# Another order of early loads, visits and blocks in a retention and squared-ReLU feed-forward kernel

## The chip, the cores and the metric

The kernel runs on one core of one Trainium2 chip. The metric is the device time of one execution in microseconds (us). The kernel before took 210.53 us, the median of 8 runs (209.96 to 211.82).

## What is computed

Eight heads of a linear recurrence with decay, then a feed-forward network on the result:

```python
gamma = 1.0 - 2.0 ** (-5.0 - np.arange(H))
for t in range(S):
    state = gamma[None, :, None, None] * state + np.einsum('bhd,bhe->bhde', k[:, :, t], v[:, :, t])
    y[:, :, t] = scale * np.einsum('bhd,bhde->bhe', q[:, :, t], state)
x = y.transpose(0, 2, 1, 3).reshape(B * S, H * D)
h = np.maximum(x @ w_in, 0.0)
out = h * h @ w_out
```

with B = 4, H = 8, S = 768, D = 64; w_in is 512 x 2048 and w_out 2048 x 512. All inputs and the output are float32; the kernel multiplies in bfloat16.

## The kernel before

**Work and its names.** The 3072 tokens are 24 chunks of 128, numbered 0 to 23, six for each batch entry. The recurrence is done by chunks, in halves of 64 tokens. What a chunk m needs is loaded by three DMAs (`ldk`, `ldq`, `ldv`, lines 436 and 616), cast to bfloat16 on whatever engine the plan gives (`ck`, `cq`), and v is scaled on VectorE (`cv`, line 627). q and k must also be transposed. Chunks 0 to 3 go in pairs (`together`, `pair_visits`, 512 KB a load, steps T, E, A, B, C); chunks 4 and 5 by TensorE with a copy out of PSUM (`Tk`, `Tq`, `Ek`, `Eq`); chunks from NPE = 6 to below NTD by `flips` inside a visit (32 transposes of 64 x 64 into the upper half of the tile `yy`, line 642, and one ScalarE copy `E`, line 648); all later ones by a DMA transpose `X` that SyncE issues (line 660).

**Visits.** A visit `Vm.n` on TensorE finishes chunk m (`values`, `apply`: tile `yy`) and begins chunk n (`scores`, `sums`: tile `sc`); `V.5` only begins, `V4.` only finishes. After it VectorE masks the scores (`Pn`, line 766), adds up the states (`Sn.0`, `Sn.1`, lines 777 and 779) and scales the result into the network's input (`Ym`, line 788, which reads `yy`). The next visit needs P and S of its m, and the transposed q and k of its n.

**The network.** `BLOCKS` groups the chunks: FFN1 of a block (`F1.b.f`, line 835) runs 64 matmuls, each 128 columns wide per chunk of the block, in groups of one PSUM bank of 512; ScalarE applies the ReLU (`R`, line 840), VectorE squares (`Q`, line 845). FFN2 of a chunk (`F2.m.0` to `.3`, line 880) runs 16 matmuls of 512 columns in four pieces; ScalarE copies the result out (`Om`, line 888) and SyncE stores it (`stm`, line 893). w_in comes in four half-blocks and two whole ones (`ldwin0` to `5`), w_out in four (`ldwout0` to `3`), each cast to bfloat16 in parts (`cw`).

**Who sets the order.** [...]each engine runs its list from first to last. The list is made while the kernel is built, by `Plan.schedule`: it places, one by one, the operation that could start earliest by its own estimates, and among equals the one of lower priority number. `ORDER` gives the loads' priorities, `HOME` fixes an operation's engine, `RANK` its priority; `LEAD` and `PACE` set how far ahead of FFN1 the visits stand, `F2LAG` how far FFN2 stands behind; `AHEAD` is how many chunks ahead a chunk's preparation is written into the plan, `PRE` a number of tiny matmuls at the start, and fillers (line 936) are matmuls on the identity put where TensorE would be idle early on. Nearly all DMAs stand in one list on SyncE's queue: loads, transposes and stores. The order of the built instructions on each engine was compared for both kernels; places in it that the next sections name come from there.

Of the kernel before, what the change touches and what calls it, by code (L numbers as in the profile page):

```python
# [18 lines left out]
class Plan:  # L19
# [12 lines left out]
    BLOCK = 256  # L32
    AHEAD = 50
    HOP = 0.15
# [6 lines left out]
    def add(self, name, eng, dur, reads=(), writes=(), fn=None, prio=0.0, lat=0.0, bank=None, after=(), count=0):  # L41
# [17 lines left out]
        else:  # L59
            flex = True  # L60
        if name in HOME:
            eng = {HOME[name]: eng[HOME[name]]}
        prio = RANK.get(name, prio)
        self.ops.append(dict(i=i, name=name, eng=eng, flex=flex, deps=sorted(deps), fn=fn,
# [3 lines left out]
    def schedule(self, nbanks, max_open):  # L68
# [18 lines left out]
        if "PE" in eng_free:  # L87
            eng_free["PE"] = 0.06 * PRE
        bank_free = [0.0] * nbanks
# [7 lines left out]
        done = 0  # L97
        issued, edge, next_fetched, history, crossed = 2 * PRE, self.BLOCK0, 3.0, [], 0.0
        while done < n:
# [54 lines left out]
            else:  # L154
                if eng == "PE":
# [9 lines left out]
                    while issued + todo > edge:  # L165
                        step = max(0, edge - issued)
                        now = max(now + step * per, next_fetched)
                        issued, todo = max(issued, edge), todo - step
                        ahead = next((y for x, y in reversed(history) if x <= edge - self.AHEAD), 0.0)
                        ahead = max(ahead, crossed)  # L170
# [5 lines left out]
                    history.append((issued, t + dur))  # L176
                    if any(before < x <= issued for x in range(self.BLOCK0 - self.AHEAD, issued + 1, self.BLOCK)):
                        behind = [x for x in moves if x[0] > t + 0.4]
# [35 lines left out]
TURN = (0.60, 1.10, 16, 2.4)  # L214
WIDE = (0.60, 2.80, 33, 0.6)
STORE = (0.30, 0.80, 9, 0.6)
BLOCKS = [2, 2, 1, 1, 2, 2, 2, 4, 4, 4]
SPLIT = 6
AHEAD = 5
WARM = 20.0  # L220
FILL = 0.215
WARMING = 18.4
PACE = 10
LEAD = 1
NPE = 6
NTD = 8
PRE = 50
WHALF = 2
WHALFD = (0.60, 1.47, 33, 0.6)
CVT = {'DVE': 0.69, 'POOL': 1.3}  # L230
TCAST = {'DVE': 0.43, 'ACT': 0.63, 'POOL': 0.78}
TEVAC = {'ACT': 0.6, 'DVE': 0.62}
NPAIR = 2
F2LAG = 5.0
F2WAIT = 4
LAST = [256, 128, 128]
CAST = {"k": {"DVE": 0.43, "ACT": 0.63, "POOL": 0.78}, "q": {"DVE": 0.43, "ACT": 0.63, "POOL": 0.78}}
# [2 lines left out]
WPRIO = {"in": -2.0, "out": 2.0}  # L240


HOME = {'cq7': 'ACT', 'ck7': 'DVE', 'ck4': 'ACT', 'cwout0.1': 'POOL', 'cwin1.0': 'ACT', 'cq0.0': 'DVE', 'Ek2.0': 'DVE', 'cwout2.0': 'ACT', 'ck2.1': 'POOL', 'cwin5.3': 'DVE', 'ck5': 'ACT', 'cq6': 'ACT', 'Eq5': 'ACT', 'cwin3.0': 'ACT', 'ck6': 'DVE', 'cwout1.0': 'DVE', 'ck0.0': 'DVE', 'cwin4.0': 'DVE', 'cwout3.3': 'ACT', 'cwin1.2': 'DVE', 'cwin5.0': 'DVE', 'Ek0.1': 'ACT', 'cwout1.2': 'POOL', 'cwin2.0': 'ACT', 'cwout0.2': 'DVE', 'cwin4.2': 'DVE', 'cwin5.2': 'POOL'}
ROUND = []
RANK = {'P0.00': -1.1, 'Tk2.1': 21.9, 'vf20': -1.1, 'B0': 1.9, 'S1': 0.9, 'Y2.0': 5.65}
ORDER = (
    "k0 q0 v0 k2 o0 q2 o1 v2 i0 i1 o2 i2 k4 i3 i4 i5 q4 v4 k5 q5 o3 q6 k6 v5 q7 v6 v7 k7"
)


# [8 lines left out]
def kernel(  # L259
# [25 lines left out]

    blocks = BLOCKS
    assert sum(blocks) == NM
# [318 lines left out]
    def prepare(m):  # L606
        if m < 2 * NPAIR:
            if m % 2 == 0:
                together(m // 2)
            return  # L610
        b, i = where(m)
        slot = m % NLD
        for x in "kqv":
            t = ld[x][:, slot, :]
            pl.add(f"ld{x}{m}", "SP", SMALL, (), (f"ld{x}{slot}",),
                   lambda x=x, t=t: nc.sync.dma_start(
                       t.rearrange("s (h d) -> s h d", h=H),
                       src[x][b, :, i * C : (i + 1) * C, :].rearrange("h s d -> s h d")),
                   prio=dma_prio[(x, m)])
        for x in "kq":  # L620
            t, o = ld[x][:, slot, :], bf[x][m % NBF]
            pl.add(f"c{x}{m}", CAST[x], 0, (f"ld{x}{slot}",), (f"bf{x}{m % NBF}",),
                   lambda on, t=t, o=o: copy_on(on, o.rearrange("s j a d -> s a j d"),
                                                t.rearrange("s (a j d) -> s a j d", a=2, j=NJ)), prio=urgency(m))
        t, o = ld["v"][:, slot, :], bf["v"][m % NBF]
        pl.add(f"cv{m}", "DVE", 0.69, (f"ldv{slot}", "vf"), (f"bfv{m % NBF}",),
               lambda: nc.vector.tensor_tensor(  # L627
                   out=o[:], in0=t.rearrange("s (h d) -> s h d", h=H),
                   in1=vf[:, i, :, None].to_broadcast([P, H, D]), op=ALU.mult),
               prio=urgency(m))  # L630
# [21 lines left out]
    def transpose(m):  # L652


        qkT, t = qkts[m % NQT], kq[m % NBF]
        if m < 2 * NPAIR or NPE <= m < NTD:
            return
        if m >= NPE:
            pl.add(f"X{m}", "SP", TURN, (f"bfk{m % NBF}", f"bfq{m % NBF}"), qkeys(m),
                   lambda: nc.sync.dma_start_transpose(out=qkT.rearrange("p x j t -> p (x j) t"),  # L660
                                                       in_=t.rearrange("s x j a d -> s (x j a d)")), prio=-0.5)
            return
        for x, name in enumerate("kq"):
            o1 = {}

            def fn(x=x, o1=o1):
                ps = fps[o1["op"]["bank_index"]].bitcast(BF16)
                for j in range(NJ):
                    nc.tensor.transpose(ps[:, j * P : j * P + P], t[:, x, j].rearrange("s a d -> s (a d)"), ident[:])  # L669
            i0 = pl.add(f"T{name}{m}", "PE", 0.26, (f"bf{name}{m % NBF}", "ident"), (f"gT{name}{m}",), fn,  # L670
                        prio=-200 + m, lat=0.2, count=4, bank=("open", ("T", m, x), False))
            o1["op"] = pl.ops[i0]
            pl.add(f"E{name}{m}", EVAC, 0, (f"gT{name}{m}",), (qkeys(m)[x],),
                   lambda on, x=x, o1=o1: copy_on(on, qkT[:, x].rearrange("p j t -> p (j t)"),
                                                  fps[o1["op"]["bank_index"]].bitcast(BF16)[:, 0:512]),
                   prio=urgency(m), lat=0.05, bank=("close", ("T", m, x)))
# [50 lines left out]
    def visit(m, n, t=None):  # L727
# [28 lines left out]
        if n is None:  # L756
            dur += 0.2
        pl.add(f"V{'' if m is None else m}.{'' if n is None else n}", "PE", dur, reads, writes, fn,
               prio=-300 + n if m is None else -300 + m if m < PACE else (m - LEAD) * 8, lat=0.25,
               count=32 * ((m is not None) + (n is not None) + (t is not None)) + 1)  # L760
# [99 lines left out]
    def ffn2(blk):  # L860
        for q4 in range(blk0[blk], blk0[blk] + blocks[blk]):
# [5 lines left out]
            for part, w in enumerate(widths):  # L867
# [5 lines left out]
                for j in range(4):  # L873
                    reads = [f"h{g % NH2}.{u}.{4 * j + c}" for c in range(4)] + [f"wout{j}.{c}.{h}" for c in range(4) for h in range(2)]

                    def mm(j=j, o1=o1, h2=h2, u=u, ns=ns, w=w):
                        ps = fps[o1["op"]["bank_index"]]
                        for c in range(4):
# [3 lines left out]
                    i0 = pl.add(f"F2.{q4}.{j}" + f"/{part}" * (parts > 1), "PE", 0.866 * w / DM, reads, (f"g{grp}",), mm,  # L882
                                prio=(q4 + F2LAG) * 8 + 2 * j + 1 + part * 9, lat=0.2,
                                bank=("open", grp, True) if j == 0 else ("use", grp), count=4)
# [18 lines left out]
    for m in range(-1, NM):  # L903
        n = m + 1
        for x in range(0 if m < 0 else m + AHEAD, min(NM, m + AHEAD + 1)):
            prepare(x)
            transpose(x)
        t = m + 2 if NPE <= m + 2 < NTD else None
        if n < 2 * NPAIR:
# [18 lines left out]
    if tc is not None:  # L928
        with tc.manual_schedule():
            one = nc.const_aps.tensor(1.0, [P, 1], BF16)  # L930
            for _ in range(PRE):
                nc.tensor.matmul(fps[NBANK - 1][0:1, 0:1], lhsT=one, rhs=one, start=True, stop=True)
# [37 lines left out]
```

## Time and profile before

| | |
|---|---|
| runs | median 210.53 us, 209.96 to 211.82, 8 runs |
| the profiled execution | 210.22 us; span of its instructions 208.4 us |
| mean granted TensorE clock | 0.992 |
| HBM read, written | 27.26 MB, 6.29 MB |
| DMA queue of the loads, stores and transposes | 80.5% of 16 engines' span |
| FFN1 matmuls (L835) | 640, of 128, 256 and 512 columns |
| FFN2 matmuls (L880) | 416 |
| transposes by DMA (L660) | 16; flips (L642): 64 matmuls |

The profile is that of one execution. Its page gives, for each engine, the busy time, then the span in 40 slices whose digits are busy tenths, then the chain of work that ended last: from the last instruction back, at each step, to what released it. PE is TensorE, PEld its weight loads, DVE VectorE, ACT ScalarE, POOL GpSimd and SP SyncE; L and a number is the line of the kernel. In a timeline a row has the start, the duration, the engine, the line, the operation, the tiles (out<-in), and in brackets how long its engine was idle before it and what ended that. When a DMA landed is seen where a waiting engine goes on with that as its releaser, and in the trace's semaphore events. Successive matmuls overlap in the profile, so a group's time is better read from its first matmul to that of the next group.

### The profile page before, as it was taken

What the parts mean: (1) busy time and instruction counts of PE and PEld (TensorE: products, weight loads), DVE (VectorE), ACT (ScalarE), POOL (GpSimd) and SP (SyncE); (2) the same over time, 40 slices, a digit from 0 to 9 for tenths busy, and PEclk for the clock granted to TensorE, in tenths of its full rate; (3) what the DMA queues carried; (4) which work ended last, traced back from release to release, by engine and by line L of the source; (5) the groups of instructions that cost most, each with busy time, mean ns of one, the idle gap of its engine ahead of it and who ended that gap; (6) DMA issues with size and microseconds to landing.
All of it is one profiled execution on the core that took longest, in us unless ns stands there. A gap on an engine that the chain in (4) does not pass through costs nothing.

```text
span 208.4 us, 6170 instructions
## 1 busy us (share of the span) xinstructions
PE 201.8 (97%) x2687; PEld 120.9 (58%) x2687; DVE 113.4 (54%) x249; ACT 91.5 (44%) x154; POOL 39.2 (19%) x67
## 2 busy tenths in 40 slices
PE   7979999999999999999999999999999999999994
PEld 5655787664484776857744444444444444444453
DVE  2597688655294684746763657935668324320000
ACT  8443777385341452533511465213653136532121
POOL 6652224310221122221302222202300000000000
PEclk9996999999999999999999999999999999999999
DMA  6999999999999999999969999889920110011212
GB/s 162 290 318 324 380 324 371 264 251 206 285 195 195 247 191 217 217 159 234 172 154 264 193 235 192 157 184 210 212 53 0 53 50 3 0 50 52 101 53 101
DMA packets 94587, 38.15 MB, mean 183 GB/s; under 512 B 79968, under 2 KB 88544, under 8 KB 94560
## 3 DMA queue, kind: packets, MB, share of 16 engines
q1 hardware_dynamic: 94416, 37.69, 80.5%
q8 instruction: 21, 0.34, 0.7%
q10 hardware_dynamic: 144, 0.07, 0.1%
q14 instruction: 6, 0.05, 0.1%
HBM read 27.26 MB, written 6.29 MB: 161 GB/s over the span
## 4 chain that ended last, share of the span: by engine, by line
PE 89%; DMA 4%; SPq 4%; ACT 1%; issue 1%; DVE 0%; POOL 0%; ACTq 0%
PE fps L835 41%; PE fps L880 40%; DMA wst<-in_moe_w_in_dram 4%; SPq L436 4%; PE yy L686 2%; PE yy L701 2%; PE sc L723 1%; PE sc L712 1%; ACT qkT L648 0%; PE fps L669 0%; PE yy L642 0%; DVE xt L788 0%; POOL w_in L421 0%; PE sc L522 0%; PE yy L522 0%
## 5 line engine op out<-in xcount | busy, mean ns | idle before, releaser
L835 PE MATMUL fps<-xt,w_in 128*128 128x256 bf16 (+2 forms) x640 | 89.0, 297 | 0.8 <-DVE xt L788 0.4
L880 PE MATMUL fps<-w_out,h 128*128 128x512 bf16 (+2 forms) x416 | 88.2, 363 | 0.0
L840 ACT ACTIVATE h<-fps 128x512 bf16<-128x512 f32 x96 | 57.3, 597 | 42.0 <-PE fps L835 41.8
L835 PEld LDWEIGHTS <-w_in 128*128 128x128 bf16 x640 | 57.3, 99 | 29.2 <-issue 0.7
L845 DVE TENSOR_TENSOR h<-h 128x512 bf16<-128x512 bf16 x96 | 42.8, 455 | 35.7 <-ACT h L840 35.5
L880 PEld LDWEIGHTS <-h 128*128 128x128 bf16 x416 | 38.0, 98 | 39.1
L888 ACT ACTIVATE osb<-fps 128x512 f32<-128x512 f32 (+2 forms) x26 | 14.7, 564 | 56.6 <-PE fps L880 56.6
L788 DVE TENSOR_TENSOR xt<-yy,yf 128x512 bf16<-128x512 f32 x20 | 13.8, 688 | 25.6 <-PE yy L701 21.8
L421 POOL CAST kqs<-kn 128x512 bf16<-128x512 f32 x16 | 10.6, 660 | 64.5 <-DMA kn<-in_k_dram 58.9
L421 POOL CAST kqs<-qn 128x512 bf16<-128x512 f32 x17 | 11.2, 660 | 22.7 <-DMA qn<-in_q_dram 20.6
L627 DVE TENSOR_TENSOR vs<-vn,vf 128x512 bf16<-128x512 f32 x20 | 13.7, 687 | 2.6 <-DMA vn<-in_v_dram 2.6
L779 DVE TENSOR_TENSOR state<-sc,state 128x256 bf16<-128x256 f32 x33 | 13.8, 419 | 0.5
L766 DVE TENSOR_TENSOR pt<-sc,cmask 128x512 bf16<-128x512 f32 x20 | 13.6, 681 | 0.3 <-PE sc L723 0.3
L701 PE MATMUL yy<-qkT,state 64*64 64x64 bf16 x296 | 9.9, 198 | 0.2
L686 PEld LDWEIGHTS <-vs 64*64 64x64 bf16 x320 | 4.2, 107 | 7.1 <-issue 7.0
L936 PE MATMUL fps<-ident 128*128 128x256 bf16 x29 | 6.8, 379 | 0.0
L686 PE MATMUL yy<-pt,vs 64*64 64x64 bf16 x320 | 6.3, 198 | 0.0
L701 PEld LDWEIGHTS <-state 64*64 64x64 bf16 x296 | 6.1, 107 | 0.4 <-PE yy L701 0.4
L723 PE MATMUL sc<-vs,kqs 64*64 64x64 bf16 x288 | 6.2, 193 | 0.0
L712 PE MATMUL sc<-qkT 64*64 64x64 bf16 x320 | 6.2, 193 | 0.0
L421 POOL CAST w_in<-wst 128x512 bf16<-128x512 f32 x6 | 4.0, 678 | 10.2 <-DMA wst<-in_moe_w_in_dram 10.2
L421 POOL CAST w_out<-wst 128x512 bf16<-128x512 f32 x6 | 4.0, 690 | 8.9 <-DMA wst<-in_moe_w_out_dram 8.9
(70 smaller groups left out, 92.3 us busy)
## 6 DMA issues: line engine op xcount, KB each, us to landing
out_dram<-osb SPq DMA_DIRECT2D x23, 256.0 KB, 2.6
kn<-in_k_dram SPq DMA_DIRECT2D x20, 256.0 KB, 4.6
qn<-in_q_dram SPq DMA_DIRECT2D x20, 256.0 KB, 4.4
vn<-in_v_dram SPq DMA_DIRECT2D x20, 256.0 KB, 4.7
wst<-in_moe_w_out_dram SPq DMA_DIRECT2D x4, 1024.0 KB, 10.3
wst<-in_moe_w_in_dram SPq DMA_DIRECT2D x4, 512.0 KB, 8.0
wst<-in_moe_w_in_dram SPq DMA_DIRECT2D x2, 1024.0 KB, 9.1
kn<-in_k_dram SPq DMA_DIRECT2D x2, 512.0 KB, 7.1
```

What stands on the lines that cost most here:

```text
L421: nc.gpsimd.tensor_copy(o, t)
L627: lambda: nc.vector.tensor_tensor(out=o[:], in0=t.rearrange("s (h d) -> s h d", h=H), in1=vf[:, i, :, None].to_broadcast([P, H, D]), op=AL ...
L686: nc.tensor.matmul(yy[L * c : L * c + L, sub, p * L : p * L + L], lhsT=vs[r, 4 * a + j, :], rhs=pt[r, a, j, :], start=(p == 0), stop=True, ...
L701: nc.tensor.matmul(yy[L * c : L * c + L, sub, p * L : p * L + L], lhsT=st[r, j, :], rhs=qkT[r, 1, j, sub * L : sub * L + L], start=False, ...
L766: lambda: nc.vector.tensor_tensor(out=pt[:], in0=sc[:, :, 0:256].rearrange("s g (p t) -> s g p t", p=NJ), in1=cmask[:, None, None, :].to_b ...
L779: f = lambda cc=cc, j1=j1, j0=j0: nc.vector.tensor_tensor(out=sts[j1][:], in0=cc, in1=sts[j0][:], op=ALU.add)
L788: lambda: nc.vector.tensor_tensor(out=xt[:, :, u * C : u * C + C].rearrange("s p (g t) -> s g p t", g=2), in0=yy[:, :, 0:256].rearrange("s ...
L835: nc.tensor.matmul(ps[:, u * n : u * n + n], lhsT=w_in_bf[j][:, cb, c * P : (c + 1) * P], rhs=xt[:, cb, cols], start=(cb == 0), stop=(cb = ...
L840: nc.scalar.activation(h2[:, f0 : f0 + per, cols], ps[:].rearrange("p (u n) -> p u n", u=per), AF.Relu)
L845: nc.vector.tensor_mul(hv, hv, hv)
L880: nc.tensor.matmul(ps[:, 0:w], lhsT=h2[:, fb, u * C : u * C + C], rhs=w_out_bf[j][:, c, ns], start=(fb == 0), stop=(fb == NFB - 1))
L888: lambda o1=o1, slot=slot, ns=ns, w=w: nc.scalar.activation(osbs[slot][:, ns], fps[o1["op"]["bank_index"]][:, 0:w], AF.Copy),
```

## The change

Only constants of the plan change. The first loads become k0 q0 v0 q2 k2 v2, then three half-blocks of w_in, then q4, w_in, k4 and so on; NTD 7 sends chunk 7 through the DMA transpose; chunks 12 to 15 become two blocks of two; the visits' lead is two chunks, a chunk is prepared four ahead, FFN2's lag is 3.5; 20 tiny matmuls at the start instead of 50; other places for casts and copies; no fixed priorities.

```diff
-BLOCKS = [2, 2, 1, 1, 2, 2, 2, 4, 4, 4]
+BLOCKS = [2, 2, 1, 1, 2, 2, 2, 2, 2, 4, 4]
 SPLIT = 6
-AHEAD = 5
+AHEAD = 4
...
-PACE = 10
-LEAD = 1
+PACE = 8
+LEAD = 2
 NPE = 6
-NTD = 8
-PRE = 50
+NTD = 7
+PRE = 20
...
-F2LAG = 5.0
+F2LAG = 3.5
...
-HOME = {'cq7': 'ACT', 'ck7': 'DVE', 'ck4': 'ACT', 'cwout0.1': 'POOL', 'cwin1.0': 'ACT', 'cq0.0': 'DVE', 'Ek2.0': 'DVE', 'cwout2.0': 'ACT', 'ck2.1': 'POOL', 'cwin5.3': 'DVE', 'ck5': 'ACT', 'cq6': 'ACT', 'Eq5': 'ACT', 'cwin3.0': 'ACT', 'ck6': 'DVE', 'cwout1.0': 'DVE', 'ck0.0': 'DVE', 'cwin4.0': 'DVE', 'cwout3.3': 'ACT', 'cwin1.2': 'DVE', 'cwin5.0': 'DVE', 'Ek0.1': 'ACT', 'cwout1.2': 'POOL', 'cwin2.0': 'ACT', 'cwout0.2': 'DVE', 'cwin4.2': 'DVE', 'cwin5.2': 'POOL'}
+HOME = {'cq7': 'DVE', 'cwin1.0': 'ACT', 'Eq0.1': 'ACT', 'cwin5.2': 'POOL', 'Ek0.0': 'ACT', 'cwin4.1': 'DVE', 'ck0.1': 'POOL', 'Eq2.0': 'DVE', 'cq0.0': 'DVE', 'cwout3.1': 'ACT', 'Eq0.0': 'ACT', 'cwout2.1': 'ACT', 'cwin4.2': 'DVE', 'cwout2.2': 'ACT', 'cq5': 'POOL', 'cwin4.0': 'DVE', 'cwout3.0': 'DVE', 'cwin0.0': 'ACT', 'cwout0.3': 'POOL', 'cwout1.0': 'DVE', 'cwout2.3': 'POOL'}
 ROUND = []
-RANK = {'P0.00': -1.1, 'Tk2.1': 21.9, 'vf20': -1.1, 'B0': 1.9, 'S1': 0.9, 'Y2.0': 5.65}
+RANK = {}
 ORDER = (
-    "k0 q0 v0 k2 o0 q2 o1 v2 i0 i1 o2 i2 k4 i3 i4 i5 q4 v4 k5 q5 o3 q6 k6 v5 q7 v6 v7 k7"
+    "k0 q0 v0 q2 k2 v2 i0 i1 i2 q4 i3 i4 k4 i5 v4 o0 q5 o1 k5 o2 o3 q6 v5 k6 v6 q7 k7 v7"
 )
```

In ORDER, i is a piece of w_in and o a piece of w_out. In the built lists SyncE's loads follow the new ORDER as written. Before, they stood as k0 q0 v0 k2 q2 v2 i0 i1 i2 k4 i3 i4 i5 q4 o0 v4 o1 o2 k5 q5 o3 q6 k6 v5 q7 v6 v7 k7, since a load whose buffer is not yet free is placed later. X7 stands on SyncE's list behind the loads of k8, q8 and v8 and the first two stores.

## The prediction

> **What bounds the kernel now.** I read the page's engine shares and its 40 slices first, then the chain of work that ended last, then the table by stage of the first 24 us, and last the timelines of VectorE and of the DMA queue around the fifth and sixth chunk. "Start to start" below means the distance between first matmuls of neighbouring pieces of work on TensorE, read from the timeline.
>
> The page, engine shares and slices (one slice is 5.2 us):
>
> ```profile
> PE 201.8 (97%) x2687; PEld 120.9 (58%) x2687; DVE 113.4 (54%) x249; ACT 91.5 (44%) x154; POOL 39.2 (19%) x67
> ...
> PEclk9996999999999999999999999999999999999999
> DMA  6999999999999999999969999889920110011212
> GB/s 162 290 318 324 380 324 371 264 251 206 285 195 195 247 191 217 217 159 234 172 154 264 193 235 192 157 184 210 212 53 0 53 50 3 0 50 52 101 53 101
> ```
>
> TensorE is full, and for the first 150 us so are the DMA engines. So two things can set the end: the sum of TensorE's work, and whatever TensorE needs that arrives late. The fourth slice has a lower clock.
>
> The chain, with the middle left out:
>
> ```profile
> 8.54 8.01 DMA wst<-in_moe_w_in_dram
> 16.60 0.62 POOL w_in L421
> 17.27 3.39 PE fps L835 x16
> ...
> 55.57 1.03 ACT qkT L648
> 56.63 0.70 DVE xt L788
> 57.37 1.95 PE fps L835 x32
> ```
>
> FFN1 cannot begin before the first half of w_in lands and is cast; from 17.27 on the chain is TensorE but for one place. At 55.57 ScalarE copies chunk 7's transposed q and k out of PSUM, and VectorE's Y5 waits for it, as the next timeline shows: 3.82 us idle. F2.4.0 starts at 55.93 and takes 0.86; F1.3.0 could follow at 56.79 and starts at 57.37: 0.58 us lost. The other lines are why Y5's engine matters: it takes its work in order, and waits for loads.
>
> ```profile
> 47.53 0.42 DVE L845 TENSOR_TENSOR h<-h 128x512 bf16<-128x512 bf16 x1
> 50.19 0.69 DVE L627 TENSOR_TENSOR vs<-vn,vf 128x512 bf16<-128x512 f32 x1 [2.25 <-DMA vn<-in_v_dram]
> 50.80 0.68 DVE L766 TENSOR_TENSOR pt<-sc,cmask 128x512 bf16<-128x512 f32 x1
> 51.40 0.41 DVE L779 TENSOR_TENSOR state<-sc,state 128x256 bf16<-128x256 f32 x1
> ...
> 56.63 0.69 DVE L788 TENSOR_TENSOR xt<-yy,yf 128x512 bf16<-128x512 f32 x1 [3.82 <-ACT qkT L648]
> ```
>
> VectorE stood until v6 landed at 50.17; P5 (L766), whose input visit V.5 had made at 48.8, came only after. V5.6 needed it at 54.12, so nobody waited.
>
> **TensorE's sum, part by part.**
> - Chunks 12 to 15 as two blocks of two instead of one of four: FFN1 turns 64 matmuls of 512 columns into 128 of 256. The chain has 52 of the first in 11.22 (216 ns each) and 72 of the second in 7.86 (109 ns): 13.81 becomes 13.98, **+0.17**. The relus and squares stay 16 of the same shape.
> - Chunk 7 by DMA: its 32 transposes leave visit V5.6, which took 0.93 start to start with them, against 0.67 for V7.8 without: **-0.26**. The ScalarE copy of 1.02 goes too, and with it Y5's wait for it: **-0.58**. What is late next there: in the built order of the changed kernel F2.3.0 and F2.3.1 (1.73) stand between V5.6 and F1.3.0, while Y5 needs about 1.1 after V5.6 and v7's scaling before it; that fits.
> - Visits moved ahead (LEAD, AHEAD, F2LAG): the same visits and groups in another order; no work.
> - 20 warm-up matmuls instead of 50, and 31 fillers instead of 29: all ahead of 17.27, hidden behind the wait for w_in. Without that cover the fillers cost 0.23 each (12 in 2.74 at the early speed); 20 now stand ahead of the first transpose, so that starts near 6.5 instead of 5.53. By FFN1 this is recovered: its gate, w_in's first half, has the same six 512 KB loads ahead of it (k2 and q2 only trade places) and lands at 16.55 again.
>
> **The first FFN1.** Before, VectorE stood from 17.02 to 18.09 for a w_in cast that was queued ahead of state S2; C2.0 ran at 20.59, after F1.0.2. In the changed order that cast is on GpSimd, S2 is done near 18.1, and C2.0 runs between F1.0.0 and F1.0.2. The stage table has the other price here:
>
> ```profile
> 16.00:18.00 2.00, 1.62 (x55) 1.33 (x54) 1.01 (x2) 0.63 (x1) 0.61 (x1) 0.88 1.12 334
> 18.00:20.00 2.00, 2.00 (x11) 1.21 (x10) 1.78 (x5) 1.23 (x2) 0.28 (x1) 0.50 1.19 289
> ```
>
> The seventh figure is the granted clock: half speed from 17.5 to 20.9, where F1.0.0 took 1.50 and F1.0.2 1.82 start to start, against 0.87 later. With it the changed order gives F1.0.0 17.3, C2.0 18.8, F1.0.2 20.1, C2.1 21.4, F1.0.4 22.1, Tq4 23.0 and F1.1.0 at 23.2, against 23.52: -0.3. [...]
>
> **The weights after that.** k4 now goes ahead of w_in's last block, q5 ahead of w_out's second, k5 ahead of its third, each a 256 KB load of about 1.05 us. By the old landings with these pieces moved: w_in's last at 29.0 instead of 27.98, cast by 30.4, read by F1.0.12 at 31.3; w_out's first at 32.95 instead of 31.85, three casts on GpSimd to 34.9, read at 36.0; its third at 40.6, cast by 42.1, read at 42.6; its last in its old place, 43.34, cast by 44.6, read at 45.2. Nothing waits, so this part is costed at nothing; its cover is 0.5 us at the third. If that goes, the next step takes it in.
>
> **The new wait, at V5.6.** From F1.1.0 to V5.6 the changed order has 13 groups of 0.873, 4 of 0.885, 12 F2 pieces of 0.864, three transpose groups of 0.22, and V.4, V4., V.5 of 0.48, 0.75, 0.74: 27.9. (The same sum for before, with three F2 pieces more, gives 54.0; it was 54.12.) TensorE would arrive at 23.2 + 27.9 = 51.1, three F2 pieces earlier in the order than before. But on VectorE the order now reads cv5, cv6, cq7, P5, S5.0: the cast of q7, on ScalarE before, stands ahead of P5. The loads after w_out's last are the same eight 256 KB pieces in another order, so I give them the old landing times by place: 44.5, 45.7 and 46.9 for q6, v5, k6, then 49.05 for v6 (q7's place before) and 50.17 for q7. Cast 0.43, P5 0.69, S5.0 0.42, and 0.15 for the signal: V5.6 at 51.85. Behind it on TensorE waits everything else, 0.75 us. A faster start only waits longer: V.5 itself needs k6, landed 46.9 and cast until 47.6, so V.5 at 47.7 or later is safe against any clock.
>
> Before, less the three F2 pieces (2.59), stood at 51.53 here. So: +0.32 at V5.6, -0.26 flips, -0.58 stall, +0.17 width = **-0.35**.
>
> **Chunk 7's transpose on the DMA queue.** The nearest row is the 16 transposes of later chunks:
>
> ```profile
> L660 SPq DMA_TRANSPOSE qkT<-kqs x16: 1237/1950/3527, 59.7 to 151.3; - x16
> ...
> DMA to landing us min/median/max: 3.1/4.1/6.3
> ```
>
> X7 is issued after the loads of k8, q8, v8 and two stores, some 53 us, by SyncE, which stays in it 1.2 to 3.5 us; st2, k9, q9, v9, X8 and all that follow on that queue move behind it. In the changed order V6.7 stands at 59.6, V7.8 at 65.55 and V9.10 at 78.5. [...] The row says more: X8 landed at 64.19, 2.1 after v9. [...] A gain is excluded, since X7 only adds to the queue. [...] From V11.12 on, by the same sums, the store that a transpose is queued behind is ready 8.6 us or more ahead of the visit, and a transpose needs about 2 to issue and 2 more to land, so the new places of stores and visits don't bite.
>
> Sum: -0.35 + 0.15 = -0.2 on a span of 208.4. The profiled execution took 210.22 around it, 0.31 under the median of 210.53; against the median, **210.3**.
>
> **Rivals.**
> - Faster: the landing dip goes. The page's GB/s has 206 in the slice 46.9 to 52.1 against 251 and 264 ahead of it; at 1.05 a load q7 would land at 49.0, P5 is done at 50.15, and V5.6 starts when TensorE arrives, 51.1: -0.43 - 0.67 = -1.1, **209.4**. For it: a stream that is only re-ordered may dip elsewhere. Against: the byte sum is the same, and X7 to X10 then meet earlier visits. Chance 0.2.
> - Slower: the DMA queue, already full, cannot absorb X7. If it costs the full 2.1 at each following arrival and the stream has no slack, X10 comes at 80.5, V9.10 waits 2.0, **212.1** (-0.35 + 2.0). For it: the DMA row of nines. Against: idle at 62 and 74 us, and st3 gives way. It decides from X10 later than 79.9. Chance 0.28.
> - No change to see, the forecast: 0.52, its own range 209.5 to 211.4 (waits from X of 0 to 0.8, the q7 landing 0.5 either way). That the early-load part does nothing by itself is inside it: the six first loads are the same bytes.
>
> A measurement here tells about 0.5% (1.05 us) from no change. Faster by over that 0.2, within it 0.52, slower 0.28. The range takes most of both rivals: 209.2 to 212.0.
>
> **What would show it.** Right: first w_in cast at 16.6 and F1.0.0 at 17.3; VectorE waiting for q_dram just ahead of P5, and TensorE idle some 0.7 just ahead of V5.6 near 51.9; no ScalarE copy at L648 in front of Y5; F1.3.0 following without a gap; 109 ns in blocks 7 and 8. Wrong: TensorE waiting by DMA transposes at V6.7 to V9.10 by over 1 us; half clock beyond 21 us; V5.6 without a wait.

## The result, and the profile after

The changed kernel takes **209.41 us**, the median of 11 runs (209.07 to 209.80). The kernel before took 210.57 in 31 runs on the same chip. The ratio is 0.9939, with a 95% interval of 0.9923 to 0.9954. The forecast was 210.3 us, range 209.2 to 212.0: the direction was its direction, the time 0.9 us above what came. Ratios and intervals leave out executions over 1.5% above the fastest of their kernel (213.81 in experiment 6), and they are not quotients of the medians.

The profiled execution took 209.42 us with a span of 207.6 (before: 210.22 and 208.4), so 0.8 of the 1.16 us lies between the two profiles. The page of the changed kernel, engine shares and slices (5.2 us each):

```profile
PE 199.3 (96%) x2691; PEld 124.0 (60%) x2691; DVE 113.0 (54%) x245; ACT 88.3 (43%) x149; POOL 44.5 (21%) x75
...
PEclk9999999999999999999999999999999999999999
DMA  6999999999999999999999999989940111011112
GB/s 161 290 315 321 348 338 327 370 213 214 231 229 204 200 254 172 197 242 233 142 252 211 170 229 218 140 191 197 222 104 0 54 51 54 0 51 52 51 54 101
```

TensorE is still full and so are the DMA engines for 150 us, but the fourth slice of PEclk has a 9 where it had a 6. The table by stage (columns: length; busy time of PE, PEld, DVE, ACT, POOL; granted clock; DMA share; GB/s) says so in numbers:

```profile
16.00:18.00 2.00, 1.06 (x36) 0.79 (x29) 1.91 (x4) 0.63 (x1) 0.61 (x1) 1.00 1.12 334
18.00:20.00 2.00, 1.93 (x38) 1.39 (x35) 1.53 (x4) 1.21 (x3) 0.68 (x2) 1.00 1.19 288
```

The first FFN1 ran at full clock in this execution: F1.0.0 took 0.98 instead of 1.50, and F1.1.0 began at 22.04 (before: 23.52, forecast: 23.2). So TensorE starts 1.48 us earlier, and yet the last FFN2 group begins only 0.72 earlier (204.38 against 205.10). The clock is not the gain: among executions with a mean granted clock of 0.996 or more the median is 210.5 for the kernel before (56 of 120, recorded beside the experiments) and 209.2 for the changed one (7 of 11). The chain of work that ended last shows where that went:

```profile
5.05 7.30 DMA kn<-in_k_dram
...
18.53 7.92 DMA kn<-in_k_dram
...
29.63 8.59 DMA kn<-in_k_dram
39.35 0.86 PE fps L880 x4
...
52.23 1.83 PE fps L880 x8
54.06 3.57 PE fps L835 x64
57.63 1.73 PE fps L880 x8
59.99 5.29 PE fps L880 x24
```

Before, the chain left the loads at 16.55. Now it stays on loads of k until 39: up to there TensorE's early start does not set the end. Nothing of L648 or L788 stands at 55 to 57 any more: the first group of F1.3 (54.06 in the chain, whose pieces begin where the one before ended; 53.90 in the timeline) follows F2.3.1 directly. The places at which TensorE stood before 39, in the timelines of PEld (the weight loads show the wait of a group whose operand is late) and PE:

```profile
26.56 0.10 PEld L835 LDWEIGHTS <-w_in 128*128 128x128 bf16 x1 [0.17 <-DVE w_in L419]
26.89 0.55 PEld L835 LDWEIGHTS <-w_in 128*128 128x128 bf16 x6 [0.24 <-DVE w_in L419]
...
30.93 0.55 PEld L835 LDWEIGHTS <-w_in 128*128 128x128 bf16 x6 [0.43 <-POOL w_in L421]
...
38.28 0.62 POOL L421 CAST kqs<-kn 128x512 bf16<-128x512 f32 x1 [0.50 <-DMA kn<-in_k_dram]
...
38.95 0.40 PE L669 MATMUL fps<-ident,kqs 128*128 128x128 bf16 x4 [0.46 <-POOL kqs L421]
```

Start to start, F1.0.8 took 1.16 instead of 0.87 (a w_in cast on VectorE), F1.0.12 1.29 instead of 0.97, which a group ahead of a visit takes (a w_in cast on GpSimd until 30.88; a_st, below, has it without the wait), F1.2.4 with Tk5 behind it 1.52 instead of 0.89 (k5 landed at 38.23, cast until 38.90). That is 0.29 + 0.32 + 0.63 = 1.24 us. (The expectation of experiment 4 counts F1.0.12 from 0.87 and has 1.34.) VectorE around V5.6, which answers to the last timeline shown of before:

```profile
48.24 0.69 DVE L627 TENSOR_TENSOR vs<-vn,vf 128x512 bf16<-128x512 f32 x1 [1.55 <-DMA vn<-in_v_dram]
50.23 0.43 DVE L419 CAST kqs<-qn 128x512 bf16<-128x512 f32 x1 [1.30 <-DMA qn<-in_q_dram]
50.58 0.68 DVE L766 TENSOR_TENSOR pt<-sc,cmask 128x512 bf16<-128x512 f32 x1
51.17 0.41 DVE L779 TENSOR_TENSOR state<-sc,state 128x256 bf16<-128x256 f32 x1
52.45 0.69 DVE L627 TENSOR_TENSOR vs<-vn,vf 128x512 bf16<-128x512 f32 x1 [0.86 <-DMA vn<-in_v_dram]
53.06 0.69 DVE L788 TENSOR_TENSOR xt<-yy,yf 128x512 bf16<-128x512 f32 x1
```

The order is as forecast: the cast of q7 (landed 50.21, forecast 50.17) stands ahead of P5, and Y5 no longer waits for ScalarE. And TensorE at V5.6:

```profile
51.31 0.32 PE L686 MATMUL yy<-pt,vs 64*64 64x64 bf16 x16
51.46 0.43 PE L701 MATMUL yy<-qkT,state 64*64 64x64 bf16 x8
51.70 0.32 PE L712 MATMUL sc<-qkT 64*64 64x64 bf16 x16
```

V5.6 begins when P5 is done (51.26) and TensorE has just arrived, not when S5.0 is done (51.59). Its first matmuls (L686) don't read the new state; at L701 it waits for S5.0, and what stands behind waits with it. The visit takes 0.85 instead of 0.67.

**The balance of the two profiles**, from F1.1.0 to the last group: before 181.58, after 182.34. Without the stall (0.58) and the flips (0.26), before has 180.74. Without the three waits (1.24) and the one inside V5.6 (0.18), after has 180.92. So TensorE's work grew by 0.18, and most of that is the 256-column matmuls: 16 groups of 0.873 in blocks 7 and 8 instead of 16 of 0.864, 0.15. The early start is worth 1.48 and the new waits cost 1.42: they nearly cancel. What is left is chunk 7's stall and flips, 0.84, and those 0.06, less 0.18.

### The profile page after: what moved, and what is told of

It is laid out like the page before. It is cut to its first block, busy times and chain, and to the rows that moved or that the text cites. A ratio compares the mean times of both kernels' runs of the same rounds, so it can differ in the third digit from the quotient of the medians.

```text
span 207.6 us, 6175 instructions
## 1 busy us (share of the span) xinstructions
PE 199.3 (96%) x2691; PEld 124.0 (60%) x2691; DVE 113.0 (54%) x245; ACT 88.3 (43%) x149; POOL 44.5 (21%) x75
## 4 chain that ended last, share of the span: by engine, by line
PE 80%; DMA 11%; SPq 6%; POOL 1%; issue 0%; ACT 0%
PE fps L880 40%; PE fps L835 33%; DMA kn<-in_k_dram 11%; SPq L809 4%; PE yy L686 2%; SPq L436 2%; PE yy L701 1%; PE sc L723 1%; PE sc L712 1%; POOL kqs L421 1%; POOL h L421 0%; PE fps L669 0%; PE yy L642 0%; ACT osb L888 0%; SPq L616 0%
## 5 line engine op out<-in xcount | busy, mean ns | idle before, releaser
L835 PE MATMUL fps<-xt,w_in 128*128 128x256 bf16 (+2 forms) x704 | 91.9, 282 | 1.1 <-ACT w_in L417 0.9
L880 PE MATMUL fps<-w_out,h 128*128 128x512 bf16 (+2 forms) x416 | 90.8, 363 | 0.0
L835 PEld LDWEIGHTS <-w_in 128*128 128x128 bf16 x704 | 62.7, 98 | 25.5 <-ACT w_in L417 1.1
L845 DVE TENSOR_TENSOR h<-h 128x512 bf16<-128x512 bf16 x96 | 44.1, 471 | 45.9 <-ACT h L840 45.5
L421 POOL CAST kqs<-kn 128x512 bf16<-128x512 f32 x20 | 13.0, 650 | 60.8 <-DMA kn<-in_k_dram 52.2
L788 DVE TENSOR_TENSOR xt<-yy,yf 128x512 bf16<-128x512 f32 x20 | 13.7, 687 | 14.2 <-PE yy L701 14.2
L627 DVE TENSOR_TENSOR vs<-vn,vf 128x512 bf16<-128x512 f32 x20 | 14.5, 723 | 6.6 <-DMA vn<-in_v_dram 6.5
L421 POOL CAST kqs<-qn 128x512 bf16<-128x512 f32 x19 | 12.4, 652 | 22.7 <-DMA qn<-in_q_dram 22.4
L779 DVE TENSOR_TENSOR state<-sc,state 128x256 bf16<-128x256 f32 x33 | 13.8, 419 | 0.5
L766 DVE TENSOR_TENSOR pt<-sc,cmask 128x512 bf16<-128x512 f32 x20 | 13.6, 681 | 0.0
L701 PE MATMUL yy<-qkT,state 64*64 64x64 bf16 x296 | 10.1, 198 | 0.2
L686 PEld LDWEIGHTS <-vs 64*64 64x64 bf16 x320 | 4.2, 107 | 7.0 <-issue 6.6
L421 POOL CAST w_in<-wst 128x512 bf16<-128x512 f32 x7 | 5.2, 751 | 8.3 <-DMA wst<-in_moe_w_in_dram 8.3
L701 PEld LDWEIGHTS <-state 64*64 64x64 bf16 x296 | 6.2, 107 | 0.5 <-PE yy L701 0.4
L686 PE MATMUL yy<-pt,vs 64*64 64x64 bf16 x320 | 6.4, 198 | 0.0
L421 POOL CAST w_out<-wst 128x512 bf16<-128x512 f32 x7 | 4.8, 706 | 7.4 <-DMA wst<-in_moe_w_out_dram 7.4
L712 PE MATMUL sc<-qkT 64*64 64x64 bf16 x320 | 6.2, 193 | 0.0
## 6 DMA issues: line engine op xcount, KB each, us to landing
wst<-in_moe_w_out_dram SPq DMA_DIRECT2D x4, 1024.0 KB, 10.2
```

Source lines behind the costliest of these rows:

```text
L421: nc.gpsimd.tensor_copy(o, t)
L627: lambda: nc.vector.tensor_tensor(out=o[:], in0=t.rearrange("s (h d) -> s h d", h=H), in1=vf[:, i, :, None].to_broadcast([P, H, D]), op=AL ...
L686: nc.tensor.matmul(yy[L * c : L * c + L, sub, p * L : p * L + L], lhsT=vs[r, 4 * a + j, :], rhs=pt[r, a, j, :], start=(p == 0), stop=True, ...
L701: nc.tensor.matmul(yy[L * c : L * c + L, sub, p * L : p * L + L], lhsT=st[r, j, :], rhs=qkT[r, 1, j, sub * L : sub * L + L], start=False, ...
L766: lambda: nc.vector.tensor_tensor(out=pt[:], in0=sc[:, :, 0:256].rearrange("s g (p t) -> s g p t", p=NJ), in1=cmask[:, None, None, :].to_b ...
L779: f = lambda cc=cc, j1=j1, j0=j0: nc.vector.tensor_tensor(out=sts[j1][:], in0=cc, in1=sts[j0][:], op=ALU.add)
```

## The experiments

Theory A (first): the gain is X7's 0.84, and the queue on which SyncE issues loads, transposes and stores gives part of it back, at V7.8 to V9.10. Rival B: the gain comes from the earlier start or from the new order of visits by itself. In every experiment each engine's list is written out as it was built, and changed only as the diff shows. Numbers like "V6.7 at 59.29" are first matmuls; all ratios are to the kernel before on the same chip.

**1. The list written out, nothing moved** (`b_pin`).

> The kernel before, with every engine's order written out as a list in place of the planner, which gives the same instructions; the base for the edits that follow. Both theories: 210.5 us, no change. The granted clock of its single executions tells apart whether the half-speed stretch at 17.5 to 20.9 us of the first profile is a trait of this order or of one execution. Arrivals theory (the end is set by TensorE's sum and by waits on loads; an earlier or later first FFN1 is swallowed by them): executions at clock 0.98 and at 1.00 lie within 0.5 us. Start theory (the changed kernel gained by reaching F1.1.0 at 22.0 instead of 23.5): executions at clock 1.00 are 1 us or more faster than those at 0.98.

Measured: 210.57 (210.24 to 211.77), ratio 1.0001 (0.9983 to 1.0019). Writing out the list costs nothing. Its profile also shows how much of a start is chance: F1.1.0 at 23.94 instead of 23.52 with the same instructions, and the last group 0.46 later too. The clocks of the single executions: a mean of 0.992 stands for one half-speed stretch of 3.4 us (before's profile), 0.983 for two (a_best's); in the profiles these lie between 12 and 24 us. b_pin has 210.5 at 1.00 (five executions), 210.6 at 0.99 (seven), 211.54 and 211.77 at 0.984 (two); the 120 of the kernel before have 210.5 (56), 210.6 (49) and 211.7 (15, at 0.984 or less). So in the old order one such stretch costs nothing, which is the arrivals theory, and two cost 1.2, which is the start theory; the changed kernel at 0.982 and 0.984 took 209.55 and 209.25.

**2. Chunk 7's transpose alone** (`b_x7`).

```diff
-NTD = 8
+NTD = 7
 SyncE:  ... ldq8 ldv8
+X7
 ScalarE: ...
-E7
```

> The kernel before with one part of the change alone: chunk 7 by DMA transpose behind the load of v8, its 32 transposes out of V5.6 and its ScalarE copy gone; all other orders as before. Arrivals theory: -0.26 for the transposes, -0.58 for F1.3.0's wait for Y5, nothing lost to the longer DMA queue: -0.84, 209.7 us, most of the measured -1.16. Start theory: the start is unchanged, so at most -0.3. If the DMA queue cannot take X7: V7.8 or V9.10 waits, 0 or slower.

Measured: 210.82 (209.97 to 211.74), ratio 1.0002 (0.9983 to 1.0020): no gain. Yet in its profile F1.1.0 to F1.3.0 took 33.01 us instead of 33.85, the 0.84 exactly, V5.6 0.67 and F1.3.0 with no gap. That execution had started late (half clock for 10.2 us, F1.1.0 at 25.15), and even so X8 landed at 66.69 for V7.8 at 66.88 and X10 at 79.70 for V9.10 at 79.73. In this profile the saving lasts to the end: F1.1.0 to the last group is 180.76 instead of 181.58, and only the start, 1.63 later, hides it. In the medians it is gone: the median span is 208.55 against 208.80, and the time outside the span (device time less span) 1.91 against 1.77.

**3. The changed kernel without X7** (`a_flip7`).

```diff
-NTD = 7
+NTD = 8
 SyncE:  ... ldv8
-X7
 ScalarE: ...
+E7   (behind V5.6)
```

> The changed kernel with that one part undone: chunk 7's 32 transposes back in V5.6, its ScalarE copy in front of Y5, X7 gone from the queue. Arrivals theory: V5.6 now also waits for k7, landed 51.3 and cast to 52.0, so it ends near 53.0 instead of 52.2, and Y5 behind the copy ends near 54.8, F1.3.0 0.1 late: +0.95, 210.4 us. Start theory: +0.26 at most, 209.7 us.

Measured: 210.59 (209.80 to 211.54), ratio 1.0003 (0.9986 to 1.0020). All that the change brings is gone: loads, visits and blocks in their new places are worth nothing here without X7. This speaks against B, though not cleanly: the price is more than the 0.84, for a reason that its PE timeline shows:

```profile
48.79 2.76 PE L880 MATMUL fps<-w_out,h 128*128 128x512 bf16 x12
52.36 0.44 PE L642 MATMUL yy<-ident,kqs 64*64 64x64 bf16 x32 [0.81 <-POOL kqs L421]
```

In the new order V5.6 comes three FFN2 pieces earlier, and the flips in it need k7, which landed at 51.64 and was cast until 52.31. V5.6 begins 1.05 later than in the changed kernel, and F1.3.0 1.41. The new order needs X7 to take k7 out of V5.6; what it would be worth without that wait was not measured.

**4. Fillers ahead of F1.1.0** (`a_fill7`): seven more matmuls on the identity, which do no work of the kernel.

```diff
 TensorE: ... Tq4
+7 fillers
 F1.1.0
```

> The changed kernel with 7 filler matmuls of 256 columns (0.11 us each, 0.78 together) put in front of F1.1.0. They do no work of the kernel and delay everything behind. Arrivals theory: swallowed, since TensorE waits 0.29, 0.42 and 0.63 us for weights and k5 between 26 and 39 us, 1.34 in all: within 0.1 of the changed kernel, 209.4 us. Start theory: +0.8, 210.2 us.

Measured: 209.99 (208.96 to 211.46), ratio 0.9973 (0.9954 to 0.9991). In the profile the start is swallowed as said: F1.1.0 at 22.94 (0.90 later), V5.6 at 51.35 (0.04 later). But the median rose by 0.6: 8 of 22 executions lie at 208.96 to 209.66, as the changed kernel does, the others from 209.87 up. The profiled execution, 210.29 us, shows a wait of 0.92 at V9.10:

```profile
78.11 0.23 PE L701 MATMUL yy<-qkT,state 64*64 64x64 bf16 x8
79.11 0.32 PE L712 MATMUL sc<-qkT 64*64 64x64 bf16 x16 [0.76 <-DMA qkT<-kqs]
```

X10 landed at 79.07, against 77.55 in the changed kernel's profile. The clock tells more: the ten executions at 0.998 or more have a median of 209.29, 0.1 over the changed kernel's at such a clock; the twelve at 0.992 or less have 210.30. So a start later by the fillers is swallowed, as one later by half clock is (a_st, below), and both together are more than the waits can take in. The start is little of the gain, and the landing of transposes is close to the visits.

**5. Stores out of the way** (`b_st`, `b_x7_st`, `a_st`): before, b_x7 and the changed kernel, each with

```diff
 SyncE:
-... st3 ... st4 ... st5 ... X10
+... X10 st3 st4 st5
```

> The control of b_x7_st: the kernel before with only the stores st3, st4, st5 moved behind X10. By A no transpose is waited for in the kernel before (X10 about 77, V9.10 at 79.4), so earlier transposes bring nothing: 210.5, within 0.3. By B, too, nothing. If this alone gives 0.6 or more, the kernel before had a wait for the queue that its profile does not show, and both are wrong.

> The kernel before with chunk 7 by DMA transpose, as in the run b_x7, and the three stores st3, st4, st5 moved behind X10 on SyncE's list. Theory A: X7 takes about 0.84 us off TensorE's path (seen between F1.1.0 and F1.3.0 of b_x7) and gives it back at V7.8 to V9.10, because the queue of SyncE brings X8 to X10 that much later. With 0.75 MB of stores out of their way X10 lands 2 to 3 us earlier (about 77), no visit waits for a transpose, and the time is 0.6 to 0.85 us below before: 209.8, ratio 0.996 to 0.997. Rival B: b_x7 gained nothing because of something outside the queue (the clock at the start, or the ScalarE copy's place taken by other work): then this is b_x7 again, 210.6 to 210.8, ratio 1.000.

> The changed kernel with st3, st4, st5 behind X10. By A the landing of X10 (77.6 to 79.1 from execution to execution, V9.10 at 78.05) is what remains of X7's price: X10 lands near 75 in every execution, V9.10 never waits, and the median falls by 0.1 to 0.4 us to 209.0 to 209.3 with the executions closer together. By B it stays at 209.4. Had the stores been needed early (a buffer that the copies O6 to O8 wait for), it is slower by 0.3 or more.

Measured: b_st 210.71, ratio 1.0003 (0.9984 to 1.0022); b_x7_st 210.48, 1.0001 (0.9984 to 1.0018); a_st 209.56, 0.9954 (0.9941 to 0.9968). The profile of b_st, at full clock, shows that the old order doesn't keep an early start either. F1.1.0 came at 22.77, 0.75 earlier than before, and the last group at 205.64, 0.54 later, for V.5 took 1.89 instead of 0.62. It waited for v5, which landed at 48.35 here and at 46.89 before (VectorE and TensorE):

```profile
48.37 0.69 DVE L627 TENSOR_TENSOR vs<-vn,vf 128x512 bf16<-128x512 f32 x1 [1.64 <-DMA vn<-in_v_dram]
...
49.11 0.31 PE L723 MATMUL sc<-vs,kqs 64*64 64x64 bf16 x8 [1.07 <-DVE vs L627]
```

X10 landed at 75.86 in a_st, as meant, and b_x7_st at V9.10 had no wait; neither became faster. A in this form falls: it isn't X10. But b_x7_st shows one wait, at V6.7 (58.76), which takes 0.93 instead of 0.63:

```profile
58.76 0.32 PE L686 MATMUL yy<-pt,vs 64*64 64x64 bf16 x16
58.91 0.23 PE L701 MATMUL yy<-qkT,state 64*64 64x64 bf16 x4
59.26 0.32 PE L712 MATMUL sc<-qkT 64*64 64x64 bf16 x16
```

The scores (L712) are the first to read chunk 7's transposed q and k, and X7 landed at 59.22. Theory C: what takes X7's gain in the old order is X7's own landing. k7 lands at 50.4 to 52.9; its cast, 2.6 to 3.7 us in SyncE and the transfer follow, so X7 is there at 58.2 to 59.4 in the profiles so far, and a V6.7 that comes earlier waits. The old order, once 0.84 faster, has V6.7 at about 58.4; the new one does the two FFN1 groups F1.3.8 and F1.3.12 ahead of V6.7 (and F2.4.0 behind it) and has it at 59.29.

a_st gives two more readings. It met half clock (F1.0.0 1.57, F1.1.0 at 23.62), its table by stage:

```profile
18.00:20.00 2.00, 1.97 (x27) 1.11 (x24) 1.06 (x3) 1.23 (x2) 0.61 (x1) 0.50 1.18 287
```

and still V5.6 began at 51.63: 1.58 us of start became 0.32. Between F1.1.0 and V5.6 it took 28.01, with none of the three waits: the forecast's sum of 27.9.

**6. One more load in the queue** (`a_ld_x8`, control `a_ld_x17`): 256 KB of k into a staging buffer that is no longer read; nothing uses it.

```diff
 SyncE: ... ldv9
+load
 X8                     (a_ld_x17: the same ahead of X17)
```

> The changed kernel with one more 256 KB load (of k's first rows into a dead staging buffer, nothing reads it) on SyncE's list just ahead of X8. It doubles the kind of price that X7 has for the queue, with nothing changed on the engines. By A the queue has no slack up to X10: X8 lands 1.0 to 1.5 later (66.4), V7.8, which stands at 65.2, waits 0.9 to 1.3, and the time rises by about 0.8 to 1.2 to 210.3 to 210.6. By the rival that idle stretches of the stream take it in: V7.8 waits at most 0.3, and the time is 209.4 to 209.7.

> The control of a_ld_x8: the changed kernel with the same extra 256 KB load on SyncE's list ahead of X17 instead of X8, at about 110 us, where the transposes land 8 us or more ahead of their visits. If the price of a_ld_x8 (1.4 us in the median) is a matter of place: no change, 209.4, within 0.3. If a load of this size costs TensorE anything by itself (memory ports, SyncE): 210 or more.

Measured: a_ld_x8 210.78 (209.56 to 213.81), ratio 1.0004 (0.9984 to 1.0024); a_ld_x17 209.40 (209.05 to 209.44), ratio 0.9948 (0.9935 to 0.9962). The same load costs 1.4 us in the median ahead of X8 (0.8 among the six executions at full clock), and nothing that five runs show ahead of X17. PE of a_ld_x8 at V6.7 and V7.8:

```profile
60.51 0.32 PE L712 MATMUL sc<-qkT 64*64 64x64 bf16 x16 [0.70 <-DMA qkT<-kqs]
...
66.38 0.23 PE L701 MATMUL yy<-qkT,state 64*64 64x64 bf16 x8
67.92 0.32 PE L712 MATMUL sc<-qkT 64*64 64x64 bf16 x16 [1.31 <-DMA qkT<-kqs]
```

The wait at V6.7 (0.89) isn't the load's: X7 was issued before it. X7's own landing, at 60.47 here, varied. Nor is the wait at V7.8 (1.47) the load's alone. SyncE stayed in X7 for 4.89 us instead of 3.35, and v9, which stands ahead of the load, landed at 66.16 instead of 64.49; X8 landed at 67.88 instead of 65.33. So 1.67 of those 2.55 us came with X7, and 0.88 with the load.

**7. V6.7's place** (`a_v67e`, `b_x7_late`), the test of C from both sides.

```diff
 a_v67e, TensorE:    ... F1.3.12
+V6.7
 F2.3.2 F2.3.3
-V6.7
 b_x7_late (from b_x7_st), TensorE: ... F1.3.4
-V6.7
 F1.3.8 F1.3.12
+V6.7
 SyncE: ... ldk9 ldq9
+X8
 ldv9 ...
-X8
```

VectorE's operations that follow V6.7 moved with it in b_x7_late.

> The changed kernel with V6.7 moved ahead of F2.3.2 and F2.3.3, 1.82 us earlier on TensorE's list; no other instruction moves. C: V6.7 arrives at 57.5, X7 lands at 58.8 to 59.0 and V6.7 starts some 0.25 later, so TensorE stands 1.2 to 1.6 us there and nothing behind gives it back but what V9.10 would have waited anyway: 210.4 to 210.9. The rival (V6.7's place does not matter, since the landing of X7 has slack): 209.4 to 209.6.

> The kernel b_x7_st (before, chunk 7 by DMA transpose, st3 to st5 behind X10) with visit V6.7 moved behind F1.3.12, two FFN1 groups (1.78 us) later, and X8 issued ahead of ldv9. New theory C: in the old order V6.7 stands at 58.4 to 58.8 once the flips and the stall are gone, while X7 lands at 59.0 to 59.4, because k7 lands at 52 to 53 and its cast, SyncE's 3 us in X7 and the transfer follow; so V6.7 waits and X7's gain of 0.84 is gone, whatever is done behind it. With V6.7 at about 60.6 it does not wait: time 0.6 to 0.85 us under before, 209.7 to 209.95, ratio 0.996 to 0.997. The rival (X7's gain is lost somewhere else on the queue or at the start): as b_x7_st, 210.5, ratio 1.000.

Measured: a_v67e 210.21 (209.60 to 210.85), ratio 0.9987 (0.9972 to 1.0001); b_x7_late 210.08 (209.39 to 211.06), ratio 0.9983 (0.9970 to 0.9995). PE of a_v67e:

```profile
57.33 0.23 PE L701 MATMUL yy<-qkT,state 64*64 64x64 bf16 x4
58.81 0.32 PE L712 MATMUL sc<-qkT 64*64 64x64 bf16 x16 [1.25 <-DMA qkT<-kqs]
```

One visit 1.8 us earlier on the list, and 1.44 us of wait, for X7 at 58.77, as C said. The profile's end came 1.06 later, the median 0.8, the low end of what was expected. In b_x7_late V6.7 (60.60) takes 0.63 and no visit waits; F1.1.0 to the last group is 180.74, before less 0.84 to the hundredth. So the old order could have X7's gain for two FFN1 groups moved ahead of V6.7, with X8 issued earlier. Of that only 0.46 shows in the time, less than expected, and the interval of its ratio overlaps that of b_x7_st. The median span tells more: it fell by 0.75 (208.05 against 208.80), where b_x7_st's had fallen by 0.35 (208.45). So by the spans C accounts for 0.40 of the 0.49 that X7 lacked. But the time outside the span was 2.00 instead of 1.78. The other two kernels with X7 in the old order have that as well (1.91 and 1.98), the changed kernel does not (1.77). What it is was not found.

**8. All waits out** (`a_best`).

```diff
-cq7 on VectorE            ... cv7 Y5
+cq7 on ScalarE            ... Y5 cv7
 TensorE: -Tk5 F2.0.1             +F2.0.1 Tk5
          -V.5 ... F2.3.0         +F2.3.0 V.5
          -F1.3.0 ... F2.3.2      +F2.3.2 F1.3.0
          -V6.7 F2.4.0 F2.4.1     +F2.4.0 F2.4.1 V6.7
 SyncE:   -ldv9 X8, ldv10 X9      +X8 ldv9, X9 ldv10;  st3 st4 st5 behind X10
```

> The changed kernel with its waits taken out, in one order: cq7 on ScalarE instead of VectorE; Y5 ahead of cv7 on VectorE; Tk5 behind F2.0.1 (0.63 of wait); F2.3.0 ahead of V.5, so that V.5 meets a landed k6 without standing; V6.7 behind F2.4.0 and F2.4.1; X8 ahead of ldv9, X9 ahead of ldv10, st3 to st5 behind X10. By C the pieces moved ahead of the pinned places (V.5, V6.7) are work taken out from behind them: V5.6 at about 51.2 with one more FFN2 piece done, so 0.6 to 1.1 us less than the changed kernel, 208.3 to 208.8, given back in part at V7.8 (X8 about 64.3 against 64.0). The rival: the loads fix the end whatever the order, 209.4.

Measured: 209.12 (208.93 to 209.70, 6 runs), ratio 0.9946 (0.9933 to 0.9958), beside 209.40 for a_ld_x17 on the same chip, which is the changed kernel but for an idle load. It beats the kernel before; that it beats the changed kernel is not shown, and the 208.3 to 208.8 did not come. The waits up to V10.11 are gone (V11.12 has one of 0.19, X12 landing at 89.09), P5 and S5.0 long done before V5.6 (VectorE's timeline, L766 and L779; V5.6 at 51.92 with one more FFN2 piece done):

```profile
49.34 0.69 DVE L766 TENSOR_TENSOR pt<-sc,cmask 128x512 bf16<-128x512 f32 x1 [0.64 <-PE sc L723]
49.95 0.41 DVE L779 TENSOR_TENSOR state<-sc,state 128x256 bf16<-128x256 f32 x1
```

F1.1.0 came at 23.05 in this execution, and from there to the last group it is 181.09 against 182.34: with the waits out, a late start takes their place. An early start would then bring the rest, but the runs don't show that. The three executions at full clock took 208.93, 209.08 and 209.46, the three at 0.983 took 209.00, 209.17 and 209.70. What holds this order at 209.1 stays open.

## Why the prediction was off by 0.9 us

The prediction gave its best chance, 0.52, to a change within 1.05 us, and its own forecast the range 209.5 to 211.4. The change was 1.16 and the time 209.41, in the class to which it gave 0.2. Its direction was earned: the two savings of 0.84 came. That the wide range held the time is luck in part, since its low end was drawn for a rival whose reason did not come true.

Right: the stall of 0.58 and the flips of 0.26 went, with nothing late behind them (b_x7: 0.84; F1.3.0 without a gap). q7 landed when said. A faster start "only waits longer" came true as well: from 21.93 to 23.62 for F1.1.0, in the profiles of the changed kernel and its variants (a_flip7 and a_best aside, which change what V5.6 needs), V5.6 stood between 51.11 and 51.63. But the place was wrong: the start is lost at the three waits before 39 us, not ahead of V5.6.

Right by the wrong value: F1.1.0 was taken at 23.2, by the row with half clock; the profiled execution met full clock and had 22.04. Both occur with the same instructions up to there (a_ld_x17: 21.93; a_st: 23.62), and neither mattered.

Wrong, by size:

- "V5.6 at 51.85", **+0.32**: the step let the whole visit wait for S5.0, where only L701 and what stands behind it do. V5.6 ended at 52.16 instead of 52.52: 0.36. Of that 0.14 is the part of the visit done ahead of the wait, 0.12 that S5.0 ended at 51.59 and not at the sum's 51.71, and 0.10 that its reader followed 0.05 behind and not 0.15. In a_st, a_v67e and a_ld_x17 (q7 at 49.7 to 50.0) it did not wait at all. The prediction had named "V5.6 without a wait" as a sign of being wrong; of this step it was.
- "Chunk 7's transpose on the DMA queue", **+0.15**: no run shows this term; it was the author's estimate. In the changed kernel's profile no visit waited for a transpose (0.00). As a mechanism it is there: 0.92 at V9.10 in a_fill7, 0.35 at V7.8 in a_st, and one more load ahead of X8 costs 1.4. In the changed kernel's profile X7 landed at 58.81, 0.93 behind v8, where v8 had landed 1.01 behind q8 (57.87 and 56.86), and X10 at 77.55, 0.50 before V9.10 began (78.05). The place that decides was passed over: the working has V6.7 at 59.6 and draws nothing from how close ahead of it X7 lands (58.81 for a visit at 59.29). In the old order that landing takes most of the gain (experiment 7).
- The end of the span: it came 3.26 behind the first matmul of the last group instead of 3.34, 0.08 that no term has. ("+0.17" for the width came: 0.15, and 0.16 to 0.18 with the rest of TensorE's work.)
- "against the median, 210.3": the 0.31 between the profiled execution and the median was carried over. Before's median execution has a span of 208.8, 0.4 more than its profile; after's has 207.6, as its profile. A start 0.4 later goes through to the end in the old order (b_pin) and is swallowed in the new one (a_fill7, a_st). Two profiles nearer to the medians show it: b_pin (span 208.9) and a_ld_x17 (207.7), whose lists are those of the two kernels but for an idle load at 110 us. There the last group comes 1.12 earlier (204.44 against 205.56). The start is 2.01 earlier and the waits are 1.60, so 0.41 of the start is kept, beside chunk 7's 0.85, less 0.14. That the median execution is like this pair is argued, not shown: at full clock the old order's start is early too, and there it lost it at V.5 (b_st).

Together: 0.36 + 0.15 + 0.08 makes the 0.6 between a forecast of -0.2 and a span of -0.8, and 0.31 the rest.

Wrong in its words, without an effect on the sum: "Nothing waits" for the weights. Two groups did, and Tk5 did for k5, 1.24 us in all, because TensorE came 1.16 earlier than assumed and because k5's cast at Tk5 was not looked at (k5 landed at 38.23, Tk5 could have run at 38.3). In a_st, with F1.1.0 at 23.62, none of them waits. And from V11.12 on the new places "don't bite": true in the changed kernel, but narrowly (X12 landed at 89.01, V11.12 began at 89.15), and no longer in a_best.

The slower rival (its sum, 210.53 - 0.35 + 2.0, is 212.2, not 212.1) needed X10 later than 79.9; it landed at 77.55, and at 79.07 in the worst profile of a kernel with the change's queue. The faster rival, 209.4, named the right time and had V5.6 start when TensorE arrives, as it did (51.31, to its 51.1), but for a reason that did not come: the landing dip did not go (213 and 214 GB/s in the slices from 41.5 to 51.9), q7 came no earlier.

## What to carry to other kernels

When a stage is held by landings, a faster start before it is worth little: here it was worth 1.48 us, and the new waits cost 1.42. Find the first landing that TensorE meets after an edit, and compare its time with the new time of that very instruction, not with the queue's later ones. A transfer that replaces work on an engine pays only if enough other work stands ahead of its first reader: here two groups of FFN1, moved ahead of one visit in the old order, decide between 0.35 and 0.75 us of span. Ask of each wait which of the instruction's parts needs it: a visit that begins with other matmuls hides part of a late state (0.14 us of V5.6 here).

## What was not expected of the hardware

TensorE's clock at the first FFN1 is a matter of the execution. In the new order it was full in the profiles of the changed kernel, a_ld_x17 and three more, halved for 3.4 us in a_st and for 6.8 in a_ld_x8 and a_best; in the old order full in b_st, halved for 3.4 us in before, b_pin and two more, and for 10.2 in b_x7, with identical instructions up to there. F1.1.0 stood between 21.93 and 23.62 in the new order, and between 22.77 and 25.15 in the old. In the 3.4 us ahead of before's half clock (14.1 to 17.5) TensorE was busy for 2.13 us; the changed kernel's profile has 2.35 in the same stretch and 1.97 from 6.9 to 10.3, and kept full clock after both. What decides was not found. And a transpose's time in SyncE and to landing is not fixed: X7, issued at 52.5 to 53.5, landed between 58.20 and 60.47, and X10 between 76.90 and 79.07 in three kernels with the same queue (a_v67e, the changed kernel, a_fill7). A load's is not either: v5 landed at 46.89 in before and at 48.35 in b_st.
